# Turned tokens of a transformer block: 16 block moves a pair on ScalarE in place of 16 SP transfers

## The chip, the cores and the metric

The kernel runs on one core of a Trainium2 chip. The metric is the device time of one execution in microseconds, lower is better. One core has TensorE (PE, matmuls), VectorE (DVE), ScalarE (ACT), GpSimd (POOL) and SyncE (SP, which here issues nearly all transfers), an on-chip memory of 128 partitions (SBUF) and the banks that matmuls write into (PSUM). A "quarter" below is 32 of the 128 partitions.

## What is computed

Attention inside chunks of 64 tokens, then a layer norm and a two-layer network with a residual, all in float32:

```python
B, H, S, D = 8, 8, 576, 64          # chunk = 64; DM = H * D = 512; hidden size 4 * DM = 2048
scores = scale * np.matmul(q_c, k_c.transpose(0, 1, 2, 4, 3))
attn = np.exp(scores - np.max(scores, axis=-1, keepdims=True))
attn = attn / (np.sum(attn, axis=-1, keepdims=True) + 1e-09)
x = np.matmul(attn, v_c)            # then heads side by side: (B, S, 512)
xn = (x - mu) / np.sqrt(var + 1e-06) * g_ln
out = x + np.maximum(xn @ w_ch1, 0.0) @ w_ch2
```

## The kernel before

The 4608 tokens are 18 pairs of 256. The first six pairs go through a plain network while the weights are loaded, converted and stored again in DRAM in recombined blocks (`wa`, `wb`, `w2d`). The other twelve go through in three units of four pairs (`unit_ffn`, u = 0, 1, 2), each unit as a seven-product (Strassen-like) multiplication on half-size blocks.

A unit has two stages on PE. The **up stage** has four quarters of 14 steps; a step is six matmuls of 512 columns (L1133) into one of four PSUM banks. Between the steps ACT copies a bank to a `snap` tile (L1139), VectorE adds a bank and a snap into `hu` (L1142), and ACT applies relu to an `hu` tile in SBUF (L1147) or straight from a bank (L1200). A bank is overwritten by a later step as soon as its reader is done. The **down stage** (`double.products`, L1048) runs 480 matmuls. Its operands are made of `hu` just ahead of it: ACT writes the high part `hx` (L944), VectorE the rest (L953, L949). From the partial sums ACT takes halves (L997) and VectorE adds the others. The weights of both stages come through a ring of six places in SBUF, filled by SP (L758, L760) as PE frees the places.

While a unit runs, the attention of the next unit's four pairs (n = 0 to 3) is woven in, at places that a table sets by hand: `PAIR_STEPS[n]` lists, in units of a sixth of a PE step, where in the unit each part of `attention` is issued, counted from `BEGINS[n]`. Eight pairs, those of units 1 and 2, are brought in this way, four during unit 0 and four during unit 1. Each engine runs its instructions in the order in which they were issued; an instruction that waits holds all those behind it on its engine.

The last parts of a pair's `attention` are these. ACT normalizes the tokens into `xg` (L502), after GpSimd has made the scale and shift. VectorE transposes all 32 x 32 blocks of `xg` in place of each other into `turned`, a tile of the `keep` pool named `x` (L509). As a block must also change its quarter of the partitions, 16 moves (i, b = 0 to 3) bring quarter i of `turned` to quarter b of the tile `rows` (L517 before and after). In units 1 and 2 `combine` then reads `rows`, from the place 392 on in the unit before (`SUMS`): ACT scales them (L835) and rounds them to the operands `xc` (L820), VectorE does the differences and the low parts.

Of the kernel before, what the change touches and what calls it, by code (L numbers as in the profile page):

```python
# [50 lines left out]

BEGINS = (4, 92, 154, 240)
PAIR_STEPS = (
# [4 lines left out]
)  # L58
SUMS = (392, 402, 414, 545, 563, 578, 590, 602, 604, 616, 628, 640, 658.5, 664, 674)
LATE = (4, 12, 76, 82, 88, 96, 104, 112)  # L60
# [43 lines left out]
def quad(i):  # L104
    return slice(32 * i, 32 * i + 32)
# [3 lines left out]
def chunk_attention_ffn(ctx: ExitStack, tc: tile.TileContext, qkv, v01, g, g_col, w, out):  # L109
    nc = tc.nc  # L110
# [172 lines left out]
    def attention(pair, xt_cols, xs, by_pe, den_by_pe, rows_of=None, pt_raw=False, by_blocks=False):  # L283
# [223 lines left out]
        if rows_of and moved:  # L507
            turned = keep.tile([P, 4, 2 * NK, 32], F32, name="x")
            nc.vector.transpose(  # L509
                out=turned.rearrange("p b a t -> p a b t"),  # L510
                in_=xg.rearrange("p j (k b f) -> p (j k) b f", k=NK, b=4),
            )
            yield
            rows_t = rows_of().rearrange("p j k t -> p (j k t)").rearrange("p (j i n) -> p j i n", j=2, i=4)
            for i in range(4):
                for b in range(4):
                    nc.sync.dma_start(  # L517
                        rows_t[quad(b), :, i], turned[quad(i), b].rearrange("p (j k) t -> p j (k t)", j=2)
                    )
                yield  # L520
            return

        if rows_of:
            rows_t = rows_of()
# [268 lines left out]
    def rows_of(i):  # L793
        if "rows" not in shared:
            shared["rows"] = [xtp.tile([P, 2, 2, NK, P], F32, name="rows", tag=f"xt{c}") for c in "hl"]
        return shared["rows"][i // 2][:, i % 2]
# [293 lines left out]
    def mix(p, engine, pool, tag, again=False):  # L1090
        both = pool.tile([P, 2, 2, DM], F32, name="mixed", tag=tag)
        his, t_ = ([both[:, i, k] for k in range(2)] for i in range(2))
        if again:
            blocks = [[his[k], t_[k]] for k in range(2)]
            for k in range(2):
                nc.sync.dma_start(both[:, :, k], w2d[2 * p + k])
            yield
        else:
            blocks = [[x[:, DM:].bitcast(F32) for x in weights(2 * p + k)] for k in range(2)]
        for k in range(2):  # L1100
            engine.tensor_tensor(out=t_[k], in0=blocks[k][0], in1=blocks[k][1], op=ALU.add)
            yield
        b11, b12, b21, b22 = (t_[k // 2][:, k % 2 * PAIR : (k % 2 + 1) * PAIR] for k in range(4))
        for k, (out, x, y, op) in enumerate((
            (b11, b12, b11, ALU.subtract), (b12, b22, b12, ALU.subtract), (b22, b11, b22, ALU.subtract),
            (b21, b21, b22, ALU.add),
        )):
            engine.tensor_tensor(out=out, in0=x, in1=y, op=op)
            if k % 2:
                yield  # L1110
        for k in range(2):
            nc.scalar.copy(his[k].bitcast(F32R), t_[k])
        yield
        for k in range(2):
            engine.tensor_tensor(out=t_[k].bitcast(F32R), in0=t_[k], in1=his[k], op=ALU.subtract)
            yield
        nc.sync.dma_start(wb[:, p], both.rearrange("p h k (a n) -> p h (k a) n", a=2))
        yield
# [122 lines left out]
    class Tokens:  # L1241
# [10 lines left out]
        def attention(self, i, by_pe=False, den_by_pe=False, pt_raw=False, by_blocks=False):  # L1252
            rows = None
            if self.t >= LEAD:
                rows = lambda: rows_of((self.t - LEAD) % 2 * 2 + i)
            return attention(2 * self.t + i, lambda: self.cols(i), xs, by_pe, den_by_pe, rows, pt_raw, by_blocks)
# [14 lines left out]
    with tc.manual_schedule():  # L1271
# [6 lines left out]
            b=mix(2, nc.gpsimd, const, "w1"), c=mix(0, nc.vector, const, "w9", True), d=mix(3, nc.gpsimd, const, "w10", True),  # L1278
# [68 lines left out]
```

## Time and profile before

| | |
|---|---|
| median of the runs | 814.53 us (814.33 to 814.57, 3 runs) |
| the profiled execution | 817.14 us |
| its span, first to last instruction | 815.4 us |
| PE busy | 803.3 us, 99% |
| VectorE busy | 610.9 us, 75% |
| ACT busy | 384.0 us, 47% |
| granted TensorE clock, mean over the span | 1.000 (2.4 GHz) |
| unit 0, unit 1, unit 2 begin at | 326.8, 492.7, 657.2 us |

The durations below are of the profiled execution. Busy PE is time in which at least one matmul is in flight, so short holes between matmuls are what to look for there; for ACT and VectorE, the idle time before an instruction, and what ended it, is written in brackets.

### The profile page before, as it was taken

To read this page: it belongs to the slowest core of one execution; us is meant where nothing else is said; L and a number is where in the kernel's file an instruction comes from. 1 tells how busy PE (TensorE), PEld (TensorE's weight loads), DVE (VectorE), ACT (ScalarE), POOL (GpSimd) and SP (SyncE) were. 2 spreads that over 40 slices of the span, in tenths; PEclk is the share of its full clock that TensorE was granted. 3 is DMA by queue.
4 is the path that set the end of the run, shared out by engine and by line. 5 is a ranking of instruction groups with operands and counts; after the bars stand their busy time and mean duration, and the time that the engine had idled before them with its cause. 6 is when DMAs were issued, how large, how long until landed. Compare 5 with 4: busy or idle time off the path is not lost.

```text
span 815.4 us, 15494 instructions
## 1 busy us (share of the span) xinstructions
PE 803.3 (99%) x6138; PEld 677.5 (83%) x6138; DVE 610.9 (75%) x893; ACT 384.0 (47%) x601; POOL 184.8 (23%) x199
## 2 busy tenths in 40 slices
PE   7999999999999999999999999999999999999998
PEld 5878888888888888888888898888888988888887
DVE  6989984687665876877888996877889932249975
ACT  4766441122334444465656554555575522345450
POOL 0111004653766975620000001300000040000000
PEclk9999999999999999999999999999999999999999
DMA  9998414976796238988879678887796677668563
GB/s 359 334 280 236 175 52 144 368 237 225 269 334 252 112 129 325 381 282 271 282 244 328 213 243 303 293 284 260 240 323 211 196 238 250 188 203 283 183 206 129
DMA packets 113928, 201.06 MB, mean 247 GB/s; under 512 B 8512, under 2 KB 75072, under 8 KB 109888
## 3 DMA queue, kind: packets, MB, share of 16 engines
q1 hardware_dynamic: 112560, 195.35, 70.0%
q0 software_dynamic: 1296, 4.72, 3.0%
q8 instruction: 49, 0.80, 0.4%
q14 instruction: 23, 0.19, 0.1%
HBM read 142.89 MB, written 48.23 MB: 234 GB/s over the span
## 4 chain that ended last, share of the span: by engine, by line
PE 91%; DMA 4%; DVE 3%; SPq 1%; issue 0%; ACT 0%; DVEq 0%
PE y L1133 28%; PE y L622 15%; PE h L598 15%; PE y L1048 12%; PE h L1048 9%; PE s L1048 6%; PE s L328 2%; PE h L436 2%; DMA wp<-wfs 1%; DMA ring<-w2d 1%; DMA qk<-qkv 1%; DMA ring<-wb 1%; PE s L436 1%; PE s L355 0%; PE s L392 0%; PE s L530 0%
## 5 line engine op out<-in xcount | busy, mean ns | idle before, releaser
L1133 PE MATMUL y<-xc,ring 128*128 128x512 f32 x1008 | 232.5, 391 | 0.0
L1133 PEld LDWEIGHTS y<-xc,ring 128*128 128x128 f32 x1008 | 188.1, 188 | 40.1 <-ACT snap L1139 0.7
L622 PE MATMUL y<-wp,hidden 128*128 128x512 f32 x564 | 137.8, 393 | 0.0
L598 PE MATMUL h<-xth,wp 128*128 128x512 f32 (+1 forms) x432 | 129.6, 370 | 1.6 <-DMA wp<-wfs 1.6
L622 PEld LDWEIGHTS y<-wp,hidden 128*128 128x128 f32 x564 | 104.4, 188 | 21.4
L1142 DVE TENSOR_TENSOR hu<-y,snap 128x512 f32<-128x512 f32 x72 | 49.0, 685 | 70.4 <-PE y L1133 35.5
L598 PEld LDWEIGHTS h<-xth,wp 128*128 128x128 f32 x432 | 78.2, 188 | 16.4 <-DMA wp<-wfs 2.0
L1048 PE MATMUL y<-ring,hx 128*128 128x512 f32 (+1 forms) x448 | 80.3, 337 | 0.0
L598 PE MATMUL h<-xtl,wp 128*128 128x512 f32 (+1 forms) x216 | 78.3, 367 | 0.0
L944 ACT ACTIVATE hx<-hu 128x1024 fp32r<-128x1024 f32 x61 | 63.6, 1059 | 31.1 <-PE h L1048 19.7
L1048 PEld LDWEIGHTS y<-ring,hx 128*128 128x128 f32 x448 | 69.6, 190 | 9.1
L611 ACT ACTIVATE hidden<-h 128x512 fp32r<-128x512 f32 (+1 forms) x53 | 28.6, 546 | 97.8 <-PE h L598 97.8
L612 DVE SCALAR_TENSOR_TENSOR hidden<-h,hidden 128x512 fp32r<-128x512 f32 (+1 forms) x53 | 33.0, 629 | 53.8 <-ACT hidden L611 53.5
L1048 PE MATMUL h<-ring,hx 128*128 128x256 f32 (+1 forms) x332 | 71.4, 319 | 0.0
L953 DVE TENSOR_TENSOR hx<-hu,hx 128x1024 fp32r<-128x1024 f32 x51 | 62.0, 1216 | 11.7 <-ACT hx L944 6.4
L1139 ACT COPY snap<-y 128x512 f32<-128x512 f32 x72 | 41.6, 588 | 58.7 <-PE y L1133 58.0
L1048 PE MATMUL s<-ring,hx 128*128 128x256 f32 (+1 forms) x236 | 59.8, 335 | 1.1 <-DMA ring<-w2d 0.5
L1006 POOL TENSOR_TENSOR x<-parts,x 128x512 f32<-128x512 f32 x16 | 20.3, 1294 | 161.9 <-DVE x L973 161.4
L1048 PEld LDWEIGHTS h<-ring,hx 128*128 128x128 f32 x332 | 52.0, 190 | 4.6
L1048 PEld LDWEIGHTS s<-ring,hx 128*128 128x128 f32 x236 | 40.4, 190 | 6.6 <-issue 2.0
L598 PEld LDWEIGHTS h<-xtl,wp 128*128 128x128 f32 x216 | 40.3, 188 | 6.6 <-ACT xtl L561 0.2
L486 POOL TENSOR_TENSOR rstd<-vare,mhalf 128x2 f32<-128x2 f32 x12 | 8.4, 698 | 138.2 <-DVE vare L485 138.2
(177 smaller groups left out, 1212.1 us busy)
## 6 DMA issues: line engine op xcount, KB each, us to landing
ring<-wa SPq DMA_DIRECT2D x84, 512.0 KB, 5.0
ring<-wb SPq DMA_DIRECT2D x48, 512.0 KB, 4.5
ring<-w2d SPq DMA_DIRECT2D x36, 512.0 KB, 4.6
raw<-w SPq DMA_DIRECT2D x15, 1024.0 KB, 7.3
out<-x SPq DMA_DIRECT2D x22, 512.0 KB, 5.8
qk<-qkv SPq DMA_DIRECT2D x18, 512.0 KB, 6.4
w2d<-wp SPq DMA_DIRECT2D x16, 512.0 KB, 7.2
wa<-parts SPq DMA_DIRECT2D x32, 256.0 KB, 4.2
```

Source lines behind the costliest of these rows:

```text
L436: nc.tensor.matmul(o_j[j][h2][cs, a, :] if den_by_pe else rows(o[h2])[cs, ja, :], lhsT=pt_sb[r, ja, c, :], rhs=v_t[j][r, a, c, :], start=T ...
L598: nc.tensor.matmul(h, lhsT=(wh, wh, wl)[m][:, ks], rhs=(xth, xtl, xth)[m][:, k, :], start=i == 0, stop=i == len(terms) - 1,)
L611: nc.scalar.activation(hh, h, AF.Relu)
L612: nc.vector.scalar_tensor_tensor(out=hl, in0=h, scalar=0.0, in1=hh.bitcast(F32), op0=ALU.max, op1=ALU.subtract)
L622: nc.tensor.matmul(sums(pairs[j // 2])[j % 2], lhsT=(hh, hh, hl)[m], rhs=(wh, wl, wh)[m], start=f == 0 and m == 0, stop=f == NF - 1 and m ...
L944: nc.scalar.activation(hh, self.split[k][2], AF.Relu if x == "1" else AF.Copy)
L953: nc.vector.tensor_tensor(out=hl, in0=x, in1=hh.bitcast(F32), op=ALU.subtract)
L1006: engine.tensor_tensor(out=x, in0=self.staged[at][:, 2 * i : 2 * i + 2], in1=x, op=ALU.add)
L1048: nc.tensor.matmul(y, lhsT=(hh, hh, hl, hh)[m], rhs=w.rearrange("p h n -> p (h n)") if m == BOTH else w[:, (0, 1, 0)[m]], start=p == 0 and ...
L1133: nc.tensor.matmul(bank, lhsT=w[:, (0, 0, 1)[m], ks], rhs=x[:, (0, 1, 0)[m], k, :], start=start and k == m == 0, stop=k == 1 and m == 2, s ...
L1139: nc.scalar.copy(out, bank)
L1142: nc.vector.tensor_tensor(out=out, in0=bank, in1=s, op=ALU.add)
```

## The change

The 16 moves of a pair become ACT copies, with source and destination as they were. They are issued in eight portions of two copies in place of four portions of four transfers, and the table puts the portions later in the unit: for n = 0, 137 to 158 after the pair's begin in place of 104 to 140, and so on. Lines of the changed kernel behind L517 have a number that is lower by one.

```diff
 PAIR_STEPS = (
-    (0, 5, 9, 14, 20, 25, 32.5, 39, 45, 50, 67, 72, 77, 85, 90, 97, 104, 116, 128, 140),
...
+    (0, 5, 9, 14, 20, 25, 32.5, 39, 45, 50, 67, 72, 77, 85, 90, 97, 137, 140, 143, 146, 149, 152, 155, 158),
...
             for i in range(4):
                 for b in range(4):
-                    nc.sync.dma_start(
-                        rows_t[quad(b), :, i], turned[quad(i), b].rearrange("p (j k) t -> p j (k t)", j=2)
-                    )
-                yield
+                    nc.scalar.copy(rows_t[quad(b), :, i], turned[quad(i), b].rearrange("p (j k) t -> p j (k t)", j=2))
+                    if b % 2:
+                        yield
```

Where the copies land in ACT's order is decided by the weave. First, ACT in the third quarter of unit 0's up stage, the kernel before, behind the last L404 copies of pair n=2's attention:

```order
L1139 COPY snap<-y 128x512
L1147 ACTIVATE hu<-hu 128x512
L1200 ACTIVATE hu<-y 128x512
L1147 ACTIVATE hu<-hu 128x512
L502 ACTIVATE xg<-x,vare,rstd 128x512 x2
```

and the changed kernel at the same place:

```order
L1138 COPY snap<-y 128x512
L517 COPY rows<-x 32x2x128 x8
L1146 ACTIVATE hu<-hu 128x512
L517 COPY rows<-x 32x2x128 x8
L1199 ACTIVATE hu<-y 128x512
L1146 ACTIVATE hu<-hu 128x512
L502 ACTIVATE xg<-x,vare,rstd 128x512 x2
```

All 16 copies of pair n=0 now stand ahead of two relus and of L502, the normalization of the pair that is one behind.

Second, ACT from the end of unit 0's up stage into its down stage, before:

```order
L1139 COPY snap<-y 128x512 x3
L944 ACTIVATE hx<-hu 128x1024
L1147 ACTIVATE hu<-hu 128x512
L502 ACTIVATE xg<-x,vare,rstd 128x512 x2
L944 ACTIVATE hx<-hu 128x1024
L1200 ACTIVATE hu<-y 128x512
L1147 ACTIVATE hu<-hu 128x512
L1200 ACTIVATE hu<-y 128x512
L944 ACTIVATE hx<-hu 128x1024 x5
L997 COPY xg<-s 128x512
L835 ACTIVATE rows<-rows,mhalf 128x16x32 x4
L944 ACTIVATE hx<-hu 128x1024
```

and in the changed kernel, in two pieces of which the second follows two L943 after the first:

```order
L1138 COPY snap<-y 128x512 x3
L517 COPY rows<-x 32x2x128 x4
L943 ACTIVATE hx<-hu 128x1024
L517 COPY rows<-x 32x2x128 x8
L1146 ACTIVATE hu<-hu 128x512
L517 COPY rows<-x 32x2x128 x4
L502 ACTIVATE xg<-x,vare,rstd 128x512 x2
L943 ACTIVATE hx<-hu 128x1024
```

```order
L517 COPY rows<-x 32x2x128 x4
L943 ACTIVATE hx<-hu 128x1024
L517 COPY rows<-x 32x2x128 x4
L943 ACTIVATE hx<-hu 128x1024
L517 COPY rows<-x 32x2x128 x8
L943 ACTIVATE hx<-hu 128x1024
L996 COPY xg<-s 128x512
L834 ACTIVATE rows<-rows,mhalf 128x16x32 x4
L943 ACTIVATE hx<-hu 128x1024
```

The 16 copies of pair n=2 stand ahead of the second `hx`, and those of pair n=3 between the fourth and the seventh.

Third, SP where unit 0 goes from the up stage to the down stage, before:

```order
L758 DMA ring<-wa 128x1024
L517 DMA rows<-x 32x2x128 x4
L758 DMA ring<-wb 128x4x256
L517 DMA rows<-x 32x2x128 x4
L758 DMA ring<-wb 128x4x256
L517 DMA rows<-x 32x2x128 x4
L758 DMA ring<-wb 128x4x256
L276 DMA out<-x 128x2x512
L758 DMA ring<-wb 128x4x256
L760 DMA ring<-w2d 128x4x256 x2
L517 DMA rows<-x 32x2x128 x8
L760 DMA ring<-w2d 128x4x256 x2
```

and in the changed kernel:

```order
L757 DMA ring<-wa 128x1024 x3
L757 DMA ring<-wb 128x4x256 x3
L276 DMA out<-x 128x2x512
L757 DMA ring<-wb 128x4x256
L759 DMA ring<-w2d 128x4x256 x6
```

The transfers of `rows` are gone from the queue, and the ring's loads follow each other.

## Rows read from the trace of the kernel before

**Rows 1.** The page's first part: busy us, share of the span and instructions of each engine.
```profile
PE 803.3 (99%) x6138; PEld 677.5 (83%) x6138; DVE 610.9 (75%) x893; ACT 384.0 (47%) x601; POOL 184.8 (23%) x199
```

**Rows 2.** The table by stage, the down stages of unit 0 and unit 1: from:to, its length, then busy us (instructions) of PE, PE's weight loads, VectorE, ACT and GpSimd, the granted clock, the DMA engines' busy share, GB/s.
```profile
412.60:492.70 80.10, 79.04 (x482) 70.44 (x480) 73.06 (x82) 46.23 (x66) 0.42 (x1) 1.00 0.78 259
578.90:657.20 78.30, 78.30 (x482) 70.54 (x480) 72.87 (x82) 46.27 (x66) 0.41 (x1) 1.00 0.75 246
```

**Rows 3.** The timeline of PE in unit 0's down stage: start, us, line, out<-in, shapes, count, and in brackets the idle time before and what ended it.
```profile
414.41 0.62 PE L1048 MATMUL s<-ring,hx 128*128 128x512 f32 x2
...
418.47 0.70 PE L1048 MATMUL s<-ring,hx 128*128 128x512 f32 x2 [0.18 <-ACT hx L944]
...
420.96 0.70 PE L1048 MATMUL s<-ring,hx 128*128 128x512 f32 x2 [0.41 <-DMA ring<-wb]
...
437.75 0.62 PE L1048 MATMUL s<-ring,hx 128*128 128x512 f32 x2
...
443.94 0.70 PE L1048 MATMUL s<-ring,hx 128*128 128x512 f32 x2 [0.47 <-DMA ring<-w2d]
```

**Rows 4.** The same of unit 1: the matmuls that answer to those at 414.41 and 437.75, the 9th and the 137th of the stage.
```profile
580.72 0.62 PE L1048 MATMUL s<-ring,hx 128*128 128x512 f32 x2
...
602.99 0.62 PE L1048 MATMUL s<-ring,hx 128*128 128x512 f32 x2
```

**Rows 5.** Line L517: SP's instructions that issue the transfers, ns min/median/max, first and last start in us.
```profile
L517 SPq DMA_DIRECT2D rows<-x x128: 585/594/1508, 354.9 to 593.4; - x128
```

**Rows 6.** SP's timeline around unit 0's change of stage (what it issues, and for how long that holds its queue), and from the view of line L758 the time to landing of the two loads issued at 413.19 and 415.17.
```profile
415.17 0.42 SPq L758 DMA_DIRECT2D ring<-wb  x1
...
417.91 6.24 SPq L517 DMA_DIRECT2D rows<-x  x8
...
425.38 5.07 SPq L517 DMA_DIRECT2D rows<-x  x8
...
DMA to landing us min/median/max: 5.1/5.4/5.7
```

**Rows 7.** Small copies: the ACT copies of line L404 (ns min/median/max), four of them in a row in ACT's timeline, and eight 32-partition transposes in VectorE's.
```profile
L404 ACT COPY pt_sb<-p_sb x64: 400/404/407, 338.6 to 568.4; 32x256 f32<-32x256 f32 x64
...
342.54 1.66 ACT L404 COPY pt_sb<-p_sb 32x256 f32<-32x256 f32 x4
...
289.79 3.59 DVE L538 STREAM_TRANSPOSE rows<-xg 32x256 f32<-32x256 f32 x8
```

**Rows 8.** ACT's timeline, up stage: the third quarter of unit 0, the fourth, and the third of unit 1.
```profile
363.47 0.63 ACT L1147 ACTIVATE hu<-hu 128x512 f32<-128x512 f32 x1
369.56 0.60 ACT L1200 ACTIVATE hu<-y 128x512 f32<-128x512 f32 x1 [5.47 <-PE y L1133]
...
370.78 1.52 ACT L502 ACTIVATE xg<-x,vare,rstd 128x512 f32<-128x512 f32 x2
...
390.86 0.60 ACT L1200 ACTIVATE hu<-y 128x512 f32<-128x512 f32 x1 [6.24 <-PE y L1133]
...
535.84 0.60 ACT L1200 ACTIVATE hu<-y 128x512 f32<-128x512 f32 x1 [5.22 <-PE y L1133]
```

**Rows 9.** VectorE's timeline in the third quarter of unit 0, and PE's from the first matmul of the step that overwrites the bank which the second of these rows reads (the sixth step of the quarter).
```profile
372.33 1.25 DVE L509 STREAM_TRANSPOSE x<-xg 128x1024 f32<-128x1024 f32 x1
...
376.28 0.65 DVE L1142 TENSOR_TENSOR hu<-y,snap 128x512 f32<-128x512 f32 x1
...
377.53 1.75 PE L1133 MATMUL y<-xc,ring 128*128 128x512 f32 x7
```

**Rows 10.** ACT's timeline from the end of unit 0's up stage into its down stage.
```profile
406.87 0.63 ACT L1147 ACTIVATE hu<-hu 128x512 f32<-128x512 f32 x1 [1.73 <-DVE hu L1142]
410.73 1.52 ACT L502 ACTIVATE xg<-x,vare,rstd 128x512 f32<-128x512 f32 x2 [3.24 <-POOL vare L489]
412.16 1.04 ACT L944 ACTIVATE hx<-hu 128x1024 fp32r<-128x1024 f32 x1
...
414.59 3.89 ACT L944 ACTIVATE hx<-hu 128x1024 fp32r<-128x1024 f32 x4
420.59 1.06 ACT L944 ACTIVATE hx<-hu 128x1024 fp32r<-128x1024 f32 x1 [2.11 <-PE h L1048]
424.73 0.59 ACT L997 COPY xg<-s 128x512 f32<-128x512 f32 x1 [3.08 <-PE s L1048]
...
431.85 1.34 ACT L835 ACTIVATE rows<-rows,mhalf 128x512 f32<-128x512 f32 x2 [1.64 <-DMA rows<-x]
...
436.21 1.99 ACT L944 ACTIVATE hx<-hu 128x1024 fp32r<-128x1024 f32 x2
```

**Rows 11.** The same of unit 1.
```profile
573.10 0.63 ACT L1147 ACTIVATE hu<-hu 128x512 f32<-128x512 f32 x1 [1.61 <-DVE hu L1142]
576.97 1.52 ACT L502 ACTIVATE xg<-x,vare,rstd 128x512 f32<-128x512 f32 x2 [3.23 <-POOL vare L489]
578.40 1.04 ACT L944 ACTIVATE hx<-hu 128x1024 fp32r<-128x1024 f32 x1
...
586.49 1.06 ACT L944 ACTIVATE hx<-hu 128x1024 fp32r<-128x1024 f32 x1 [1.77 <-PE h L1048]
589.97 0.59 ACT L997 COPY xg<-s 128x512 f32<-128x512 f32 x1 [2.43 <-PE s L1048]
...
599.79 1.99 ACT L944 ACTIVATE hx<-hu 128x1024 fp32r<-128x1024 f32 x2
```

6 rows, old and new, of the table PAIR_STEPS are left out of this document.

## Prediction

> **What bounds the kernel now.** Start with the page's first line: TensorE (PE) is busy for 803.3 of 815.4 us, ScalarE (ACT) for 384.0 [rows 1]. So no other engine's total matters; what matters is whether PE has to wait somewhere, and a new wait is lost time, because nothing later in the program is idle enough to give it back. The next view is the table by stage: the down stage of unit 1 takes 78.30 us with PE busy throughout, the same 480 matmuls in unit 0 take 80.10 us with 79.04 busy [rows 2]. Where the difference lies is read from PE's timeline: in unit 0 there are short holes before the matmuls at 418.47, 420.96 and 443.94, the last two put down to transfers into the ring [rows 3]. From 414.41 to 437.75 unit 0 takes 23.34 us; the same stretch of unit 1, 580.72 to 602.99, takes 22.27 [rows 3, 4]. So the first two holes cost 1.07 us, and the third the rest of the 1.80.
>
> **What is removed: 128 transfers on SP.** Each keeps SP for 0.594 us [rows 5], so the 16 of a pair keep it for 9.5 us, and SP issues the ring's loads in the same queue. At 417.91 and 425.38 eight of them at a time hold the queue for 6.24 and 5.07 us; the ring load issued at 415.17, behind earlier ones, is the one that PE waits for at 420.96 (the two loads of that moment took 5.1 and 5.7 us to land) [rows 6, 3]. SP's rows in the changed order have no transfer between these loads. I take the whole 1.80 us as gained. The bounds: nothing (if the transfers are late by themselves, since 0.78 of the DMA engines' time is busy in that stage [rows 2]), and 1.80, because unit 1 and unit 0 do the same work there and unit 1 has no hole to close.
>
> **What is added: 128 copies on ACT.** The trace has the same form: L404's ACT copies move 32 partitions x 256 f32 between quarters of SBUF, 404 ns each; four in a row take 1.66 us, that is 0.415 each, with no overlap [rows 7]. So a pair's 16 copies take 6.64 us. Bounds for the spacing: ACT's large instructions do overlap, four of 1.05 us in 3.89, so 0.10 us less per instruction [rows 10]; that would give 0.31. Upwards, VectorE's 32-partition transposes of the same size take 3.59 us for eight, 0.45 each [rows 7]. I take 0.415: it is the same engine, size, and change of quarter. The Trainium skill (ScalarE: Activation LUTs, What ACT_TABLE_LOAD costs) gives 186 ns + 0.833 ns an element, an estimate of 399 ns here, which the 404 ns bear out, and says that back-to-back ACTIVATEs overlap by about 93 ns; by that a pair would take about 5.0 us and the whole sum would end as rival 1 does. The row for L404 speaks against it, and so does another page for VectorE (VectorE: DVE Perf Modes, Two Vector instructions with no wait between them): an instruction that starts in another quarter of the partitions than the one before is held until that one has finished. No row shows it for ScalarE by itself, but L404's copies, each of which writes another quarter than the one before, behave like that.
>
> The copies cost PE nothing as such. They matter where they stand in ACT's queue ahead of something that PE wants. Four places a unit:
>
> *Copies of pair n=0, third quarter of the up stage.* They stand before and after a relu of 0.63 us that can start at 363.47. After it ACT is idle until 369.56, 5.47 us [rows 8]. 364.10 + 6.64 = 370.74: 1.2 us too long. Queued behind are two more relus and then L502. The relus need 1.03 us (0.6 each, and an overlap of 0.10 each as ACT's large instructions show it [rows 10]), and 1.22 us passed between 369.56 and L502 at 370.78 [rows 8], so 0.2 is slack and L502 is 1.0 us late. VectorE waits for L502 with the transpose at 372.33 and has its next seconds full, so the addition L1142, which ends at 376.93, ends at about 377.93 [rows 9]. It empties the PSUM bank that PE's next step starts to overwrite at 377.53 [rows 9]: **0.4 us** lost. In unit 1 the idle time is 5.22 us [rows 8], 0.25 less: **0.65**.
>
> *Copies of n=1, fourth quarter.* ACT is idle for 6.24 us before 390.86 [rows 8], and PE, already 0.4 late, makes it 6.64. Nothing.
>
> *Copies of n=2, end of the up stage.* Idle time here is 1.73 and 3.24, together 4.97 us, so ACT is 1.67 late at the L944 that started at 412.16 (it splits off the high part of the down stage's second operand) [rows 10]. It ended at 413.20, now at 414.87; PE multiplies by it at 414.41 [rows 3]. **0.46** lost. In unit 1: idle 1.61 + 3.23, late by 1.80, end 578.40 + 1.04 + 1.80 = 581.24 against 580.72 [rows 4, 11]: **0.52**.
>
> *Copies of n=3, in the down stage.* By now 32 copies, 13.28 us, stand against ACT's idle time. In unit 0 that is 1.73 + 3.24 + 2.11 + 3.08 + 1.64 = 11.80 us (the last one was itself a wait for the old transfers, which is gone) [rows 10], so the L944 at 436.21 is 1.48 late, and 0.4 more because PE started the stage late. It ended at 437.26 (1.05 us [rows 10]), now at 439.14. PE wants it at 437.75 [rows 3], moved by +0.4 and +0.46 and, since the first two ring holes are gone, by -1.07: 437.54. **1.6 us** lost. In unit 1 the idle time is 1.61 + 3.23 + 1.77 + 2.43 = 9.04 us [rows 11]; the L944 of 599.79 is 4.24 + 0.65 late and ends at 605.73; PE wants it at 602.99 [rows 4] + 0.65 + 0.52 = 604.16. **1.57** lost. Behind that instruction PE is late enough that ACT catches up.
>
> What else moves: 'combine' no longer waits for transfers, a gain already counted as the 1.64; VectorE, PE and GpSimd keep their order; the `keep` tile of the turned tokens is held longer, but the next tile to take its place comes two pairs later.
>
> **Sum.** Unit 0: 0.4 + 0.46 + 1.6 = 2.46; unit 1: 0.65 + 0.52 + 1.57 = 2.74; together 5.2 lost, 1.8 gained: +3.4 us. The profiled execution took 817.14 us (815.4 of span and 1.7 around it), 2.6 above the median of the runs, so some of its waits may be weaker in a plain run; I add the difference to the median: 814.53 + 3.4 = **817.9 us**. The sum is steep in the spacing of copies: each late ns counts 16 times in the first wait and 32 times in the last, in each unit, so 10 ns of spacing are 1 us of the kernel. At 0.45 it would be +6.8; it crosses zero near 0.38.
>
> **Rivals.** 0.2% is 1.6 us, about what a measurement of this kernel can tell from no change.
> 1. *The copies overlap like ACT's large instructions.* At 0.31 a pair takes 5.0 us: less than the 5.47 and 5.22 idle at the first place, 0.0 to 0.1 too long at the third (PE had 1.2 us of slack there), and 9.9 against 11.80 and 9.04 at the last, where the L944 of 599.79 had 2.2 us of slack. No wait is left, and the ring's 1.80 us is a pure gain: 812.7 us, faster. This is what the ScalarE page's overlap would make of the kernel. For it speaks that the four L944 overlap; against it, that not one L404 does. It decides below 0.36 us a copy.
> 2. *Something between.* Four copies in a row read the same quarter and change only the output's. At 0.36 to 0.40 the waits eat up the ring's gain: 813 to 816 us, no change. L404's copies in a row change the output's quarter too, which speaks against it.
> 3. *The ring holes stay.* Then PE's holes at 418 to 444 come from slow transfers and not from SP's queue, or a plain run has none to cure: 814.53 + 5.2 = 819.7. Against it: unit 1, with the same transfers, has none, and SP was visibly the late one.
>
> **How the numbers follow.** My forecast 0.55 (own range 816.2 to 820), rival 1 0.17, rival 2 0.16, rival 3 0.12. Faster 0.17, same 0.16, slower 0.67. The range must reach down to rival 1 and up past rival 3: 812.7 to 820.5, which leaves out about half of rival 1 and the dear end of the copies, some 0.15.
>
> **What would show it.** In the profile of the changed kernel: L517 on ACT, 128 times, about 404 ns, eight in a row over 3.3 us (under 2.6 is rival 1). SP without L517; the holes before 420.96 and 443.94 gone (if not, rival 3). New waits of PE: on L1141 of VectorE in the third quarter of units 0 and 1 (0.4 and 0.65), and on ACT's L943 twice in each down stage, about 0.5 some 2 us into it and 1.6 some 25 us into it; both down stages about 80.4 us long. I would be wrong if ACT's queue had room that the idle times don't show, or if PE read the operands later than I placed them.

## The result: 0.8 to 0.9% slower, twice what was forecast

The changed kernel took 821.56 us (median, 821.17 to 823.9) beside 814.5 us for the kernel before in the same session; the ratio is 1.0087, with a 95% interval of 1.007 to 1.0104. That is +7.1 us where the forecast was +3.4, and above the range. The profiled execution took 822.04 us, its span is 819.8.

The page's first part, changed kernel: busy us, share of the span and instructions of each engine.

```profile
PE 806.1 (98%) x6138; PEld 677.4 (83%) x6138; DVE 611.7 (75%) x893; ACT 435.4 (53%) x729; POOL 184.5 (22%) x199
```

Against [rows 1] ACT has 128 instructions and 51.4 us more, that is 0.40 us a copy. ACT is still idle for nearly half of the span, and the kernel is slower all the same. The totals do not tell why, but the table by stage does. Both down stages of the changed kernel (from:to, length, busy us of PE, its weight loads, VectorE, ACT, GpSimd; clock, DMA share, GB/s):

```profile
412.57:493.51 80.94, 79.54 (x481) 70.43 (x480) 73.05 (x82) 54.31 (x84) 0.29 (x1) 1.00 0.68 222
580.67:661.65 80.98, 79.54 (x481) 70.42 (x480) 73.05 (x82) 54.35 (x84) 0.29 (x1) 1.00 0.65 209
```

Unit 0 went from 80.10 to 80.94, and unit 1, which had no hole before, from 78.30 to 80.98 [rows 2]. What PE waited for in the units, over both (us in total, times, the longest):

```profile
PE s L1047 <- ACT hx L943: 2.7, 4, 0.9
PE y L1132 <- ACT hu L1199: 0.2, 1, 0.2
PE y L1132 <- DVE hu L1141: 0.2, 1, 0.2
```

And PE's timeline: every matmul of the units ahead of which it shows an idle time.

```profile
414.97 0.73 PE L1047 MATMUL s<-ring,hx 128*128 128x512 f32 x2 [0.43 <-ACT hx L943]
438.80 0.73 PE L1047 MATMUL s<-ring,hx 128*128 128x512 f32 x2 [0.91 <-ACT hx L943]
542.23 3.02 PE L1132 MATMUL y<-xc,ring 128*128 128x512 f32 x12 [0.22 <-ACT hu L1199]
545.42 8.48 PE L1132 MATMUL y<-xc,ring 128*128 128x512 f32 x36 [0.17 <-DVE hu L1141]
583.10 0.73 PE L1047 MATMUL s<-ring,hx 128*128 128x512 f32 x2 [0.45 <-ACT hx L943]
606.94 0.74 PE L1047 MATMUL s<-ring,hx 128*128 128x512 f32 x2 [0.91 <-ACT hx L943]
```

These are the 9th and the 137th matmul of each down stage, the two named in the forecast. In each down stage they add up to 1.34 to 1.36 us, half of what it lost; the other half is in PE's busy time, 79.54 against 78.30, where no idle time is listed. When PE runs through, a row of two matmuls is 0.62 us long and the next begins some 0.45 us after it, so rows overlap by 0.16 us; a gap of 0.43 us between two rows is therefore a delay of 0.59. The ring holes of [rows 3] are gone. SP's timeline shows the six loads of `w2d` in one group, with no transfer of `rows` between:

```profile
410.01 14.94 SPq L759 DMA_DIRECT2D ring<-w2d  x6
```

ACT's timeline shows the queue behind these waits: the third quarter of unit 0's up stage, then the change of stage.

```profile
362.77 3.31 ACT L517 COPY rows<-x 32x256 f32<-32x256 f32 x8
366.10 0.63 ACT L1146 ACTIVATE hu<-hu 128x512 f32<-128x512 f32 x1
366.74 3.31 ACT L517 COPY rows<-x 32x256 f32<-32x256 f32 x8
...
371.23 1.51 ACT L502 ACTIVATE xg<-x,vare,rstd 128x512 f32<-128x512 f32 x2
...
406.81 3.31 ACT L517 COPY rows<-x 32x256 f32<-32x256 f32 x8
...
410.77 1.65 ACT L517 COPY rows<-x 32x256 f32<-32x256 f32 x4
...
413.87 1.04 ACT L943 ACTIVATE hx<-hu 128x1024 fp32r<-128x1024 f32 x1
...
423.70 3.31 ACT L517 COPY rows<-x 32x256 f32<-32x256 f32 x8
...
430.92 1.05 ACT L943 ACTIVATE hx<-hu 128x1024 fp32r<-128x1024 f32 x1
...
437.70 2.00 ACT L943 ACTIVATE hx<-hu 128x1024 fp32r<-128x1024 f32 x2
```

Eight copies take 3.31 us, 0.414 each: the price taken from L404 was right, and nothing overlaps. From 403.4 to 439.6 ACT's timeline shows no idle time at all. The `hx` that PE takes up at 414.97 starts at 413.87 and ends at 414.91 (forecast 414.87); that of 437.70 ends at about 438.7 (forecast 439.14).

### The profile page after: what moved, and what is told of

Its sections match the earlier page's. It is cut to its first block, busy times and chain, and to the rows that moved or that the text cites. A ratio compares the mean times of both kernels' runs of the same rounds, so it can differ in the third digit from the quotient of the medians.

```text
span 819.8 us, 15438 instructions
## 1 busy us (share of the span) xinstructions
PE 806.1 (98%) x6138; PEld 677.4 (83%) x6138; DVE 611.7 (75%) x893; ACT 435.4 (53%) x729; POOL 184.5 (22%) x199
## 4 chain that ended last, share of the span: by engine, by line
PE 76%; ACT 14%; DVE 5%; DMA 3%; issue 2%; SPq 0%; ACTq 0%; DVEq 0%
PE y L1132 17%; PE y L621 15%; PE h L597 15%; PE y L1047 10%; PE h L1047 8%; PE s L1047 5%; ACT rows L517 4%; ACT hx L943 2%; PE s L328 2%; ACT pt_sb L404 2%; ACT snap L1138 1%; DMA wp<-wfs 1%; ACT rows L834 1%; ACT xg L502 1%; PE h L436 1%
## 5 line engine op out<-in xcount | busy, mean ns | idle before, releaser
L1141 DVE TENSOR_TENSOR hu<-y,snap 128x512 f32<-128x512 f32 x72 | 49.1, 685 | 69.6 <-PE y L1132 34.7
L943 ACT ACTIVATE hx<-hu 128x1024 fp32r<-128x1024 f32 x61 | 64.0, 1061 | 28.1 <-PE h L1047 18.3
L517 ACT COPY rows<-x 32x256 f32<-32x256 f32 x128 | 51.6, 403 | 1.6
```

What stands on the lines that cost most here:

```text
L517: nc.scalar.copy(rows_t[quad(b), :, i], turned[quad(i), b].rearrange("p (j k) t -> p j (k t)", j=2))
L943: nc.scalar.activation(hh, self.split[k][2], AF.Relu if x == "1" else AF.Copy)
L1141: nc.vector.tensor_tensor(out=out, in0=bank, in1=s, op=ALU.add)
```

## The experiments

The table gives, for each profiled execution, the length of the up and down stages in us (from the first matmul of one to the first of the next) and the time from the start of unit 0 to the end. Unit 2's stages agree within 0.05 us everywhere. Before unit 0 the executions differ by up to 3.4 us, whatever the kernel, so the last column says more than the span. "Copies" says where those of n=0,1 / n=2 / n=3 run.

| kernel | copies | up u0, u1 | down u0, u1 | unit 0 to end | plain runs: ratio to before |
|---|---|---|---|---|---|
| before | SP | 85.77, 86.21 | 80.11, 78.29 | 488.55 | |
| before, again | SP | 85.80, 86.15 | 79.86, 78.29 | 488.28 | |
| changed | ACT | 86.44, 87.16 | 80.94, 80.98 | 493.67 | 1.0087 [1.007, 1.0104] |
| changed, again | ACT | 86.53, 87.14 | 80.91, 80.95 | 493.67 | 1.008 [1.0066, 1.0094] |
| no moves | none | 85.77, 86.16 | 78.30, 78.29 | 486.67 | 0.9984 [0.9972, 0.9996] |
| GpSimd | GpSimd | 85.83, 86.26 | 79.53, 79.52 | 489.27 | 1.002 [1.0011, 1.0028] |
| half | ACT and VectorE | 89.15, 89.51 | 78.30, 78.29 | 493.39 | 1.0064 [1.005, 1.0078] |
| GpSimd early | GpSimd | 86.07, 87.00 | 79.43, 79.42 | 490.05 | 1.0028 [1.0017, 1.0039] |
| n=2, n=3 | none / ACT / ACT | 85.79, 86.18 | 80.93, 80.95 | 492.0 | one run |
| n=3 | none / none / ACT | 85.78, 86.43 | 79.19, 79.12 | 488.67 | one run |
| split | GpSimd / GpSimd / both | 85.83, 86.23 | 78.29, 78.29 | 486.79 | 0.9993 [0.9982, 1.0003] |

**The kernel before, again.** No edit.

> The kernel before, unchanged, profiled a second time. Theory A, the ring holes belong to the kernel (SP's queue is late in every execution): unit 0's down stage again takes about 80.1 us, 1.8 longer than unit 1's, with PE waiting for ring loads near 418, 421 and 444 us, and the execution again takes about 817 us. Theory B, they belong to the one execution that was profiled (817.14 us against a median of 814.5): both down stages take 78.3 us, no hole, span near 812.8.

Measured: 816.33 us. The first down stage is again longer than the second, by 1.57 us, but of the three holes only the last came back, and larger. PE's timeline, the only gap of that stage:

```profile
443.21 0.70 PE L1048 MATMUL s<-ring,hx 128*128 128x512 f32 x2 [1.13 <-ACT hx L944]
```

It is the 169th matmul of the stage, the same one as at 443.94 in [rows 3]. The view puts the gap down to an `hx` of ACT, but in the first profile that L944 runs from 443.51 to 444.57, and the same matmul begins at 443.94: it doesn't need it. What fits is a ring load. The `w2d` load issued at 432.25 lands at 443.07 here, and the one issued at 433.34 landed at 443.81 in the first profile, each 0.13 to 0.14 us ahead of the matmul. SP's queue stands for 5.08 us on eight transfers of `rows` from 424.27, ahead of the last `w2d` loads, and that load takes 10.8 us to land (10.5 in the first profile). In the kernel without moves below, the same load is issued 3.3 to 3.8 us earlier in the stage and takes 6.1. So the transfers make it late twice, in the queue and on its way; how the two share the hole is not shown. Theory A holds for the 1.6 to 1.8 us that unit 0 loses in a profiled execution, but not for the holes near 418 and 421.

**No moves.**

```diff
-                    nc.scalar.copy(rows_t[quad(b), :, i], turned[quad(i), b].rearrange("p (j k) t -> p j (k t)", j=2))
```

> The changed kernel with the 128 copies left out, so that the units 1 and 2 work on stale tokens: neither copies on ScalarE nor transfers on SP. Theory A (the ring holes cost 1.8 us in plain runs too): 812.7 us, 0.2% below before. Theory B (they do not): 814.5, the same as before, and then all of the changed kernel's loss of 7.1 us is the copies'. Both theories: both down stages 78.3 us, no wait of TensorE on L943, L1141 or L1199 in units 0 and 1.

Measured: 814.38 us beside 815.33, ratio 0.9984 [0.9972, 0.9996]. The table by stage, both down stages:

```profile
413.89:492.19 78.30, 78.30 (x482) 70.56 (x481) 72.87 (x82) 46.28 (x66) 0.42 (x1) 1.00 0.70 230
578.35:656.64 78.29, 78.29 (x481) 70.56 (x480) 72.87 (x82) 46.19 (x66) 0.41 (x1) 1.00 0.67 217
```

The ratio's interval holds theory A's gain of 1.8 us and leaves out theory B's of nothing. PE is never idle in these stages. This is the floor, and against it the changed kernel loses 493.67 - 486.67 = 7.0 us: 0.67 and 1.00 in the up stages, 2.64 and 2.69 in the down stages. The whole ring gain is 1.88 us against the first profile of the kernel before and 1.61 against the second, and 0.3 to 2.3 us by the interval of plain runs, with 1.3 in the middle.

**The copies on GpSimd, at the same places.**

```diff
-                    nc.scalar.copy(rows_t[quad(b), :, i], turned[quad(i), b].rearrange("p (j k) t -> p j (k t)", j=2))
+                    nc.gpsimd.tensor_copy(rows_t[quad(b), :, i], turned[quad(i), b].rearrange("p (j k) t -> p j (k t)", j=2))
```

> The 16 copies of a pair by GpSimd at the same places. If ScalarE's queue is the cause of the loss, all of TensorE's waits on L943, L1141 and L1199 go and the time falls to that of the kernel without moves, 812.7 to 814.5 us, as long as GpSimd's copies (its 128x512 additions take 1.3 us; half the columns would be about 0.65 an instruction, 10 us a pair) don't hold up the scale and shift of the next pair. If they do (the scale of pair n=2 is made about 6 us after the first copy of n=0), L502 is late instead by several us and the time is 816 to 820. If the loss is due to the moves as such (SBUF traffic), it stays near 821.5.

Measured: 817.17 us, ratio 1.002 [1.0011, 1.0028]: most of the loss goes away with ACT's copies. The up stages are within 0.1 us of the floor; the down stages keep 1.2 us each, half of it in one wait of PE for L943 (0.6 us). The time is in the range of the second branch of the expectation, but not for its reason: L502 is not late. GpSimd ends the copies of n=3 at 430.93, ACT has stood idle for 2.83 us for them at L834, and the `hx` behind that instruction are late.

**Half on ACT, half on VectorE.**

```diff
-                    nc.scalar.copy(rows_t[quad(b), :, i], ...)
+                    if b % 2:
+                        nc.vector.tensor_copy(rows_t[quad(b), :, i], ...)
+                    else:
+                        nc.scalar.copy(rows_t[quad(b), :, i], ...)
```

> Eight of a pair's copies on ScalarE, eight on VectorE, as L404 does it. ScalarE's share is 3.3 us a pair, less than its idle time at each place (5.47, 5.22, 4.97, 4.84), so by the theory of the queue its waits go; VectorE's share is 2.4 us (0.30 each), and it is idle for about 5 us of each down stage and 17 of each up stage. Queue theory: 813 to 815.5 us. If the loss does not hang on the idle time but on the number of copies ahead of a waited-for instruction, half of it stays: 818.

Measured: 821.04 us, ratio 1.0064 [1.005, 1.0078]; the expectation failed. The down stages are at the floor, so ACT with half the copies is no longer late there. But each up stage lost 3.3 us. PE's waits in the units, then VectorE ahead of one of them:

```profile
PE y L1135 <- DVE hu L1144: 3.0, 4, 1.3
PE y L1135 <- ACT hu L1202: 1.1, 2, 0.6
```

```profile
411.09 0.58 DVE L518 COPY rows<-x 32x256 f32<-32x256 f32 x2
411.70 0.69 DVE L1144 TENSOR_TENSOR hu<-y,snap 128x512 f32<-128x512 f32 x1
```

The addition L1144 that empties a bank ends at 412.39; PE goes on at 412.45 after 1.26 us of waiting. Five copies of 0.29 us stand in VectorE's queue in the 6.2 us ahead of that addition. The waits for ACT's L1202, 1.1 us over both units, come on top. It is the mistake of adding ACT work by its mean idle time once more, with VectorE: one engine has room in the down stage, the other in the up stage, and each was loaded in both.

**The changed kernel, again.** No edit.

> The changed kernel, unchanged, in more rounds on the same chip as the next one. By the traces its units 0 and 1 lose 6.6 us of waits and gain the 1.6 to 1.8 us of ring holes: 5 us, ratio 1.006. By the first comparison 7.1 us, ratio 1.0087. If plain runs of the kernel before have the hole as its two profiles do, it is 1.006; if they mostly have none, 1.008 or more.

Measured: 822.02 us beside 815.6, ratio 1.008 [1.0066, 1.0094]. Every stage is within 0.1 us of the first profile. The interval leaves out the ratio of 1.006 that the traces alone gave; a part of the rest lies outside the span (see below). The waits of the changed kernel are fixed, those of the kernel before are not.

**GpSimd, as soon as a pair is turned.** The edit of GpSimd above, and earlier places in the table:

```diff
-    (..., 97, 137, 140, 143, 146, 149, 152, 155, 158),
-    (..., 80, 126, 129, 132, 135, 138, 141, 144, 147),
-    (..., 105, 148, 151, 154, 157, 160, 163, 166, 169),
-    (..., 91, 113, 117, 121, 125, 129, 133, 137, 141),
+    (..., 97, 100, 102, 104, 106, 108, 110, 112, 114),
+    (..., 80, 83, 85, 87, 89, 91, 93, 95, 97),
+    (..., 105, 108, 110, 112, 114, 116, 118, 120, 122),
+    (..., 91, 94, 96, 98, 100, 102, 104, 106, 108),
```

> All 128 copies on GpSimd, each pair's placed right behind its transpose and so ahead of the next pair's scale and shift in GpSimd's queue. Theory: in the run with GpSimd at the changed kernel's places TensorE waited only because pair n=2's copies stood behind the scale of n=3 and pushed those of n=3 into the down stage; with that order gone both down stages take 78.3 us, the up stages 85.8 and 86.2, and the time is that of the kernel without moves, 0.1 to 0.2% below before (ratio 0.998). Rival: GpSimd's copies, 0.48 us each, hold up the scale of the next pair and with it L502, or slow VectorE down while they run: ratio 1.002 to 1.004.

Measured: 817.89 us, ratio 1.0028 [1.0017, 1.0039]: no better than at the late places. The theory failed in both stages: the down stages keep 1.13 us each, and the up stages, 86.07 and 87.00, are 0.30 and 0.84 over the floor. What the up stages wait for was not followed. GpSimd's timeline, the copies of n=2 and of n=3:

```profile
394.29 6.92 POOL L517 COPY rows<-x 32x256 f32<-32x256 f32 x16 [2.97 <-DVE x L509]
...
415.15 16.23 POOL L517 COPY rows<-x 32x256 f32<-32x256 f32 x16 [4.99 <-DVE x L509]
```

The same 16 copies take 6.92 us in one place and 16.23 in the other, and in the second ACT has to wait for them, with `hx` behind that wait in its queue:

```profile
431.42 1.34 ACT L834 ACTIVATE rows<-rows,mhalf 128x512 f32<-128x512 f32 x2 [2.73 <-POOL rows L517]
```

**Without the copies of n=0 and n=1; only those of n=3.**

```diff
+                    if (0, 2, 1, 3)[(pair - 10) % 4] in (2, 3):
                         nc.scalar.copy(rows_t[quad(b), :, i], ...)
```

and with `in (3,)` for the second.

> The changed kernel with the copies of pairs n=0 and n=1 left out (their rows stay stale); those of n=2 and n=3 on ScalarE as before. If the places add up as taken: up stages 85.8 and 86.2 us (no wait on L1141 or L1199), both down stages unchanged at 80.8.

> Only the copies of pair n=3, in the down stage (the other pairs' are left out). ScalarE has 1.7 + 2.4 us of idle time behind them for 6.64 us, so it is 2.4 late at the later L943s. If TensorE waits for ScalarE alone, the L943 that it needs 25 us into the stage had 2.2 us of slack: 0.2 to 0.3 lost, down stage 78.6. If VectorE carries the delay on (it runs without a gap from 19 us into the stage to its end), it is 2.4 late to the end, 1.7 of that is slack there, and the loss is about 0.75, at the last product: 79.0 to 79.1.

Measured: 818.93 and 816.69 us, one run each. Without n=0 and n=1 the up stages are back at the floor and the down stages stay at 80.93 and 80.95, so each part of the loss belongs to the pairs that it was put down to. (The up stages of the changed kernel lose only in the third quarter, where n=0's copies stand; the fourth, with those of n=1, loses nothing, as forecast.) With n=3 alone the down stages are:

```profile
411.57:490.76 79.19, 78.92 (x482) 70.57 (x480) 73.05 (x82) 52.58 (x82) 0.29 (x1) 1.00 0.70 227
577.19:656.31 79.12, 78.93 (x481) 70.57 (x480) 73.04 (x82) 52.51 (x82) 0.28 (x1) 1.00 0.66 214
```

That is 0.8 to 0.9 above the floor, near the 0.75 of the theory in which VectorE carries the delay on, and above the 0.2 to 0.3 of the other; but only 0.35 of it comes at the last product, and about 0.5 at the 137th matmul. The n=2 copies, whose last ends 0.15 us before the stage begins (410.77 + 1.65 against 412.57), add 1.8 of the 2.65 us to that; by themselves they were not run. (Unit 1's up stage is 0.25 us longer here, with one wait of 0.2 us on a `snap`; why is open.)

**Each copy where an engine is idle.** n=0 and n=1 on GpSimd at the places of the change, n=2 on GpSimd just after it is turned, n=3 half and half:

```diff
-    (..., 105, 148, 151, 154, 157, 160, 163, 166, 169),
+    (..., 105, 108, 110, 112, 114, 116, 118, 120, 122),
...
+                    if b % 2 and (pair - 10) % 4 == 3:
+                        nc.scalar.copy(rows_t[quad(b), :, i], half)
+                    else:
+                        nc.gpsimd.tensor_copy(rows_t[quad(b), :, i], half)
```

> The copies go where an engine is idle while they run: those of n=0 and 1 to GpSimd at the places of the change, those of n=2 to GpSimd just after their transposition (at about 394 us, while VectorE leaves GpSimd 0.43 us a copy), and of n=3 eight to GpSimd (1.3 us each beside VectorE in the down stage, 10 us from about 415, over before ACT asks for the tokens at about 428) and eight to ACT (3.3 us, less than the 1.7 us of slack and the idle time there take up together). By my theory: up stages within 0.3 us of 85.8 and 86.2, both down stages 78.3 to 78.5, no ring hole, so the level of the kernel without moves, a ratio of 0.998 to 0.9995 to the kernel before. Rival, GpSimd's copies slow VectorE so much (1.22 to 1.41 us an instruction) that VectorE's lateness alone passes its slack: down stages 79 or more, ratio 1.000 to 1.002.

Measured: 814.6 us (813.51 to 815.9) beside 815.3 (813.29 to 818.38), ratio 0.9993 [0.9982, 1.0003]. In the trace it is what the first theory said; the table by stage:

```profile
410.94:489.23 78.29, 78.29 (x481) 70.56 (x480) 74.02 (x82) 49.64 (x74) 10.85 (x9) 1.00 0.69 230
575.46:653.75 78.29, 78.29 (x481) 70.56 (x480) 74.02 (x82) 49.65 (x74) 10.85 (x9) 1.00 0.68 217
```

PE has no hole although all the moves are done, and GpSimd's eight slow copies have made VectorE 1.15 us busier, which its slack takes up. From unit 0 to the end it is 6.9 us shorter than the changed kernel. To the kernel before, the interval still contains no change.

One thing was not run: ACT's copies at the places that the transfers had. How much of the loss the later places in the table carry is not shown.

## Why the prediction was wrong

The step that failed is the one that let a down stage's loss end at the 137th matmul. The prediction followed ACT's delay to PE and had nothing behind it; the runs show that VectorE takes over the same delay and keeps it to the end of the stage, so that a down stage loses 2.64 and 2.69 us where 2.06 and 2.09 were forecast. Beside it, the up stages lose 1.67 us in place of 1.05, and the gain in plain runs is smaller than the 1.8 us of the one profile.

**Right: the price of a copy, and the place of the two large waits.** 0.414 us against 0.415, and the 9th and the 137th matmul. Rivals 1 and 2 needed copies of under 0.40 us. The Trainium skill's overlap of about 93 ns between back-to-back ACTIVATEs (ScalarE: Activation LUTs, What ACT_TABLE_LOAD costs) does not appear in these 32-partition copies, which begin 0.414 us after each other and last 0.404.

**Right: the mechanism of the up stage, wrong: that it takes effect once.** VectorE's timeline there, the changed kernel:

```profile
372.77 1.25 DVE L509 STREAM_TRANSPOSE x<-xg 128x1024 f32<-128x1024 f32 x1 [1.06 <-ACT xg L502]
...
376.64 0.65 DVE L1141 TENSOR_TENSOR hu<-y,snap 128x512 f32<-128x512 f32 x1
```

Counted from the start of unit 0 (326.13 here, 326.82 before), L502 is 1.14 us late (45.10 against 43.96; forecast 1.0) and the end of L1141 1.05 (51.16 against 50.11 [rows 9]); PE's sixth step of the third quarter begins 0.51 late (forecast 0.4). But the lateness meets other steps too: in unit 0 the steps 3 to 6 of that quarter lost 0.10, 0.13, 0.28 and 0.13, and in unit 1, 0.38, 0.14, 0.33 and 0.13. The first of these is the relu L1199, 0.22 us in PE's timeline at 542.23: it too empties a bank that PE wants, and it had been put down as slack because only the way through L502 was followed. The stages lost 0.67 and 1.00, forecast 0.4 and 0.65.

**Right for ACT, wrong for the stage: "Behind that instruction PE is late enough that ACT catches up."** ACT does: against the kernel without moves, its L943 at 437.70 begins 4.34 us later in the stage, the one at 455.84 only 2.29, no later than PE itself. But measured from the pattern of unit 1 before [rows 4], a down stage loses 0.72 us at the 9th matmul and just behind it (forecast 0.46 and 0.52), 0.36 between the 97th and the 113th (forecast 0; the L943 of 430.92 is late), 1.22 at the 137th (forecast 1.6) and 0.35 at the last product (forecast 0). The 0.72 is more than the 0.43 of the gap: the 9th matmul starts 0.59 later than in unit 1 before, and the matmuls after it lose another 0.13. The loss at the end shows what was overlooked. VectorE in the kernel without moves:

```profile
425.16 1.22 DVE L947 SCALAR_TENSOR_TENSOR hx<-hu,hx 128x1024 fp32r<-128x1024 f32 x1
...
482.38 1.22 DVE L951 TENSOR_TENSOR hx<-hu,hx 128x1024 fp32r<-128x1024 f32 x1
...
490.95 0.69 DVE L971 TENSOR_TENSOR x<-h,x 128x512 f32<-128x512 f32 x1 [1.48 <-PE h L1046]
```

and the same three in the changed kernel:

```profile
428.12 1.23 DVE L948 SCALAR_TENSOR_TENSOR hx<-hu,hx 128x1024 fp32r<-128x1024 f32 x1 [1.94 <-ACT hx L943]
...
485.39 1.23 DVE L952 TENSOR_TENSOR hx<-hu,hx 128x1024 fp32r<-128x1024 f32 x1
...
492.40 0.69 DVE L972 TENSOR_TENSOR x<-h,x 128x512 f32<-128x512 f32 x1
```

Counted from the start of the stage (413.89 and 412.57), VectorE's first row stands at 11.27 and at 15.55, 4.28 us late, because it waits for `hx` behind ACT's copies; 57 us later, at 68.49 and 72.82, it is 4.33 late. In between it makes up nothing: until 18.8 us into the stage (23.1 in the changed kernel) its idle times are waits for ACT's `hx`, which is late as well, and from there to the additions of the last product (L971 at 490.95) it has none. [rows 2] hinted at it, with 72.87 us of work in the 78.30 of unit 1. So it is not ACT, but VectorE that cannot catch up, and it hands the delay to the last product, whose bank `h` it empties late. VectorE's and PE's rows of the changed kernel there:

```profile
481.33 0.75 DVE L1000 TENSOR_TENSOR parts<-h,parts 128x256 f32<-128x256 f32 x2
```

```profile
481.80 3.23 PE L1047 MATMUL h<-ring,xg 128*128 128x256 f32 x24
```

PE overwrites `h` from 481.80 on, 0.10 us after the middle of the two additions (481.33 + 0.75 / 2), when the first has just read its part. With n=3's copies alone VectorE is 2.60 us late in the same way, and unit 0's stage 0.89 longer; with all of them 4.34 and 2.64. In both cases 1.7 us of VectorE's lateness are free.

The other profiles say the same. In all twelve down stages of units 0 and 1 in which the copies make VectorE late (the changed kernel twice, GpSimd, GpSimd early, n=2 and n=3, n=3 alone), the first addition that reads `h` for `parts` begins 2.53 to 4.36 us later in its stage than without moves, and the stage is longer by 1.68 to 1.71 us less than that. With the half and the split kernel this addition is not late, and the stages lose nothing. PE's wait at the 137th matmul goes with the same delay: behind it PE is 2.02 to 2.06 us less late than VectorE in each of the twelve, and the last 0.34 to 0.36 us come at `h`. In unit 0 of the two profiles of the kernel before, VectorE is late there too, by 2.82 and 2.23 us, but PE, held by the ring, is itself 1.81 and 1.57 late; the difference is only 1.0 and 0.7, and nothing is lost at `h`. No run delayed VectorE without making ACT's `hx` late, so the part of VectorE by itself is read from these rows and was not tried.

**Mis-sized: the gain in plain runs.** 1.80 us stood in one profiled execution and 1.57 in the next, and the kernel without moves gained 1.88 and 1.61 on them in its trace. In plain runs it gained about 1.3 (0.3 to 2.3), and the split kernel, whose stages are as clean, 0.6 (from 1.5 gained to 0.2 lost). The remark that waits may be weaker in a plain run stood in the sum, with no number taken off for it.

A part of this lies where the prediction counted nothing: in the time of a run that is not in its span from the first to the last instruction. It is 1.73 to 1.82 us in all runs of the kernel before that list their span, the "1.7 around it" of the prediction, but 2.1 to 2.3 in the changed kernel and without moves, and 2.0 to 2.1 in the split one. So the changed kernel loses 0.45 us there, and the gains of the other two, read from the median spans, are 1.45 and 1.0 us. Why this time grows was not tried. Whether the ring holes come in every plain run is not shown either: in the last session the kernel before spread from 813.29 to 818.38, the split one from 813.51 to 815.9.

**The sum again.** Lost: 0.67 + 1.00 + 2.64 + 2.69 = 7.0 us, not 5.2. Gained in plain runs 0.6 to 1.3, with the time around the span in it, not 1.8. That gives +5.7 to +6.4, inside both measured intervals (+5.7 to +8.5 and +5.4 to +7.7 us). Of the error of 3.7 us, 1.8 lie in the waits and 0.5 to 1.2 in the gain, of which 0.3 to 0.5 are outside the span; 0.7 to 1.4 are not settled. Against the second comparison, +6.4 us, nothing to 0.7 is left.

## What to carry to other kernels

An engine's idle time is worth something only at the place in its queue where the new work stands; list there everything that is queued behind, and follow each of it to the instruction that wants it, not only the one way that looks longest. Then ask which engine downstream has no idle time left to lose a delay in (here VectorE, 73 of 78 us in the down stage): a delay that reaches it stays until the stage ends. A hole in one profiled execution that comes from traffic need not be worth as much in the median of plain runs; a second profile of the same kernel tells whether it stands still. And compare the time around the span as well: a change can move it, here by 0.45 us.

## What was not expected of the hardware

GpSimd's copy of 32 partitions x 256 float32 takes about 0.43 us from start to start (16 in 6.92) while VectorE runs its mixture of the up stage, and 1.01 on average (16 in 16.23) in the down stage beside VectorE's instructions with two inputs in SBUF. The split kernel shows both in one trace:

```profile
393.33 7.07 POOL L521 COPY rows<-x 32x256 f32<-32x256 f32 x16 [2.97 <-DVE x L509]
...
413.94 10.82 POOL L521 COPY rows<-x 32x256 f32<-32x256 f32 x8 [4.99 <-DVE x L509]
```

There it is 1.35 us a copy. VectorE pays as well: in the kernel with early GpSimd copies, beside those of n=3, an instruction that takes 1.22 us otherwise takes 1.41:

```profile
417.62 1.41 DVE L952 TENSOR_TENSOR hx<-hu,hx 128x1024 fp32r<-128x1024 f32 x1
```

The Trainium skill (SBUF — State Buffer, SBUF: two separate sides) says that a VectorE operation with two SBUF inputs and a GpSimd operation that reads SBUF exclude each other on a port pair that they share, and that the one that comes second waits for the whole of the other. The 0.43 and 1.35 us agree with such an exclusion; but VectorE's instructions become longer by only 0.19 us, half of what a GpSimd copy takes by itself, so VectorE was not held for the whole of one here. VectorE's own copy of that size takes 0.29 us, ACT's 0.40.
